# Block transposes on VectorE for denominators and clusters, a third weight buffer, and two held feed-forward pieces

## The chip, the cores and the metric

One core of a Trainium2 chip runs the whole program. The metric is the device time of one execution in microseconds, the median of several; smaller is better.

## What is computed

Two stages follow each other. The first is attention with cluster routing: 4 batches, 8 heads, 768 tokens, head size 64, 16 centroids per head. Every query and every key belongs to the cluster whose normalised centroid is nearest, and a query sees only the keys of its own cluster:

```
q_assign = argmax(q_n . c_n);  k_assign = argmax(k_n . c_n)
scores   = q k^T / sqrt(64), only where q_assign == k_assign
attn     = softmax(scores);  attn_out = attn v
```

The second stage is a feed-forward layer over the 3072 tokens, with a slope per hidden unit for negative values:

```
x = attn_out as (4*768, 512)
h = x @ w_in                                  # 512 -> 2048
g = max(h, 0) + alpha * min(h, 0)
out = g @ w_out                               # 2048 -> 512
```

The weights w_in and w_out arrive as 64-bit floats and are turned into fp32 on the chip; everything large is fp32.

## The kernel before, in words

The work is cut into 96 steps (`steps`, L313). The order is by batch, then by half of the queries (384 columns), then by pair of heads (4 pairs), then by group of two key tiles (3 groups, s = 0, 1, 2). The 12 steps of one (batch, half) are called a block here: block 0 is steps 0 to 11, block 7 steps 84 to 95, and after step 95 comes a tail. The order of all instructions is written out by hand in the loop at L498, and each engine executes its own part in that order.

What one step u puts out, in this order:

- `score(u)`: four score products into PSUM (L327, 8 TensorE instructions, since an fp32 product is two passes), then two exponentials on ScalarE (L335) into the tiles E, keys on partitions.
- `weigh(u-1)`: the products of the masked E with v, summed over the keys in PSUM tile vps (L388). At a pair's last step (s = 2) it first adds up the denominators: `sum_rows` (L368) multiplies by a matrix of ones, so that each row of the result holds the sum over all keys, repeated on 64 partitions. VectorE takes the minimum of it (L403) and the reciprocal (L405) over 128 x 384 elements.
- `mask(u)`: four VectorE instructions (L343) that compare the cluster of each query (tile aq, the query's cluster number repeated on all partitions) with the cluster of each key (a column of tile first) and multiply E by the result.
- `normalise(u-1)`: at s = 2, xT = vps * rd (L413), which writes one of the four chunks of xT, the input of the feed-forward layer.
- `add_up(u)`: from block 1 on, VectorE adds the masked E tiles into acc (L356, L361), so that `sum_rows` has one source instead of six. In block 0 `sum_rows` takes E itself.
- Then feed-forward pieces of the block before, preparation pieces of later pairs and weight conversions, interleaved one by one (L523).

Feed-forward pieces (`ffn_pieces`): per block 16 `hidden(f)` (8 instructions L434, two ScalarE instructions L441 and L442; a VectorE instruction L426 for the slope is issued with the next hidden piece) and 12 `final` (8 instructions L453 each; 8 instructions are 4 products). 28 pieces are spread over the 12 steps of the next block, 3 or 2 per step; the last block's pieces are the tail. In the pieces for the first block, four hidden pieces and three final ones alternate, because the weights are being converted at the same time; in all others, hidden pieces come first. Each `hidden` reads all four chunks of xT. Their PSUM tiles come from the pool ps_f, which has two buffers.

Preparation of a pair (only for half = 0, in the steps before it is needed): three steps ahead, transposes of q and k (`prep_features`, L241, copied by ScalarE at L245); two steps ahead, similarities with the centroids (`prep_sims`, L268, copied by ScalarE into simT, L273) and then `prep_clusters`: three TensorE transposes (L279), and VectorE finds for each token the highest similarity and the first cluster that reaches it (L285 to L294). One step ahead, and for both halves, `prep_queries` broadcasts the clusters of the queries to all partitions: three bf16 products with the identity per head (L304) and a ScalarE copy into aq (L307).

Weights (`convert`, L169): 32 pieces of 128 x 512 numbers. SP issues the transfer into a tile raw (pool raws, two buffers), VectorE takes exponent and mantissa apart (L176, L178), ScalarE converts them (L180, L182), and one conversion later VectorE completes both (L186, L189) and GpSimd multiplies them into w_in_sb or w_out_sb (L192). One conversion is issued in each of steps 1 to 11, two in each of steps 12 to 23; `convert_up_to` adds some if a feed-forward piece needs its weights sooner.

At the end a flag is computed from the largest squared norm and the smallest denominator (L531 to L541, one product at L538); TensorE has that product in its queue before the tail's pieces.

Of the kernel before, what the change touches and what calls it, by code (L numbers as in the profile page):

```python
# [21 lines left out]
def kernel(  # L22
# [43 lines left out]
    rdp = fast.enter_context(tc.tile_pool(name="rdp", bufs=2))  # L66
# [49 lines left out]
    ident_bf = const.tile([P, P], BF16, name="ident_bf")  # L116
    nc.gpsimd.tensor_copy(out=ident_bf, in_=ident)
# [15 lines left out]
    csq = const.tile([P, D], FP32, name="csq")  # L133
    cs2 = const.tile([P, 1], FP32, name="cs2")
    nc.vector.tensor_tensor(out=csq, in0=cen, in1=cen, op=ALU.mult)
    nc.vector.tensor_reduce(out=cs2, in_=csq, axis=AX.X, op=ALU.add)
# [6 lines left out]
    cn = const.tile([P, D], FP32, name="cn")  # L143
# [109 lines left out]
    NG, W = 4, 2 * NC  # L253
    GT = NB // NG
    assert NB % NG == 0 and W * NG == P and GT * P <= 512

    def slot(t, h):

        g, i = divmod(t, GT)
        return (i * NG + g) * 2 + h  # L260

    simTs = {}

    def prep_sims(n):
        hp = pairs[n][1]
        ps = misc()
        for g in range(NG):
            nc.tensor.matmul(out=ps[g * W:(g + 1) * W, 0:GT * P],  # L268
                             lhsT=cT[:, hp * W:(hp + 1) * W],
                             rhs=qkTs[n][:, g * GT * P:(g + 1) * GT * P],  # L270
                             start=True, stop=True)
        simTs[n] = asg.tile([P, GT * P], FP32, name="simT")
        nc.scalar.copy(simTs[n], ps[:, 0:GT * P])  # L273

    def prep_clusters(n):
        simT = simTs.pop(n)
        ps = misc()
        for i in range(GT):
            nc.tensor.transpose(out=ps[:, i * P:(i + 1) * P],  # L279
                                in_=simT[:, i * P:(i + 1) * P], identity=ident)  # L280
        sim = ps[:, 0:GT * P].rearrange("p (t c) -> p t c", c=NC)


        mx = asg.tile([P, 2 * NB], FP32, name="mx")
        nc.vector.tensor_reduce(out=mx, in_=sim, axis=AX.X, op=ALU.max)  # L285
        top = asg.tile([P, 2 * NB, NC], BF16, name="top")
        nc.vector.tensor_tensor(
            out=top, in0=sim, in1=mx[:, :, None].broadcast_to((P, 2 * NB, NC)),
            op=ALU.is_ge)
        nc.vector.tensor_tensor(  # L290
            out=top, in0=top, in1=rank[:, None, :].broadcast_to((P, 2 * NB, NC)),
            op=ALU.mult)
        first = fsp.tile([P, 2 * NB], BF16, name="first")
        nc.vector.tensor_reduce(out=first, in_=top, axis=AX.X, op=ALU.max)  # L294
        firsts[n] = first

    def prep_queries(n, half, h):

        if h == 0:
            aqs[n, half] = aqp.tile([P, 2, HS], BF16, name="aq")  # L300
        ps = misc()
        for i in range(HJ):
            t = slot(half * HJ + i, h)
            nc.tensor.matmul(out=ps[:, i * P:(i + 1) * P],  # L304
                             lhsT=firsts[n][:, t:t + 1].broadcast_to((P, P)),
                             rhs=ident_bf, start=True, stop=True)
        nc.scalar.copy(aqs[n, half][:, h, :], ps[:, 0:HS])  # L307
# [11 lines left out]
    def score(u):  # L319
        n, half, s = steps[u]  # L320
        qkT, first = qkTs[n], firsts[n]
# [16 lines left out]
    def mask(u):  # L338
        n, half, s = steps[u]
        for c, E in zip(range(s * GROUP, (s + 1) * GROUP), Es[u]):  # L340
            for h in range(2):
                t = slot(NJ + c, h)
                nc.vector.scalar_tensor_tensor(  # L343
                    out=E[:, h, :], in0=aqs[n, half][:, h, :],
                    scalar=firsts[n][:, t:t + 1],
                    in1=E[:, h, :], op0=ALU.is_equal, op1=ALU.mult)

    def add_up(u):
# [5 lines left out]
        if s == 0:  # L354
# [3 lines left out]
            E = E[2:]  # L358
        for e in E:
            acc = accs[n, half]  # L360
            nc.vector.tensor_tensor(out=acc, in0=acc, in1=e, op=ALU.add)  # L361

# [9 lines left out]
    def weigh(u):  # L372
# [6 lines left out]
        den = None  # L379
# [10 lines left out]
        if den is None:  # L390
            return
        if s == 0 or u >= UB:
            rds[n, half] = rdp.tile([P, HS], FP32, name="rd")
        rd = rds[n, half]
        if u < UB:
            if s == 0:
                nc.vector.tensor_copy(out=rd, in_=den[:, 0:HS])
            else:
                nc.vector.tensor_tensor(out=rd, in0=rd, in1=den[:, 0:HS], op=ALU.add)
            den = rd  # L400
        if s == SB - 1:
            i = 2 * n + half
            nc.vector.tensor_reduce(out=lowest[:, i:i + 1], in_=den[:, 0:HS], axis=AX.X,  # L403
                                    op=ALU.min)
            nc.vector.reciprocal(out=rd, in_=den[:, 0:HS])  # L405
# [89 lines left out]
    for piece in prep_at.pop(-1):  # L495
        piece()
    ffn = deque()
    for u in range(NS + 1):  # L498
# [5 lines left out]
        if u > 0:  # L504
            weigh(u - 1)
        if u < NS:
# [14 lines left out]
        take = len(ffn) - whole * (UB - 1 - u % UB) // UB if ffn else 0  # L521
# [179 lines left out]
```

## Time and profile before

| | |
|---|---|
| median of 3 runs | 1154.46 us (1152.25 to 1156.92) |
| the profiled execution | 1159.15 us |
| its span, first to last instruction | 1157.3 us |
| mean granted TensorE clock | 0.972 |
| TensorE busy | 1089.4 us, 94% |
| VectorE busy | 627.7 us, 54% |
| ScalarE busy | 390.8 us, 34% |
| GpSimd busy | 45.8 us, 4% |
| chain that ended last, by engine | PE 79%, DVE 12%, DMA 4%, ACT 3% |

PE is TensorE's products, PEld its weight loads, DVE VectorE, ACT ScalarE, POOL GpSimd, SP the engine that issues most transfers. Busy time of PE is modelled: products are pipelined, one overlaps the next, and the duration of a row of several instructions includes that overlap. The cost of a group on a full TensorE is therefore best read as the distance from its start to the start of what follows.

### The profile page before, as it was taken

What the parts mean: (1) busy time and instruction counts of PE and PEld (TensorE: products, weight loads), DVE (VectorE), ACT (ScalarE), POOL (GpSimd) and SP (SyncE); (2) the same over time, 40 slices, a digit from 0 to 9 for tenths busy, and PEclk for the clock granted to TensorE, in tenths of its full rate; (3) what the DMA queues carried; (4) which work ended last, traced back from release to release, by engine and by line L of the source; (5) the groups of instructions that cost most, each with busy time, mean ns of one, the idle gap of its engine ahead of it and who ended that gap; (6) DMA issues with size and microseconds to landing.
All of it is one profiled execution on the core that took longest, in us unless ns stands there. A gap on an engine that the chain in (4) does not pass through costs nothing.

```text
span 1157.3 us, 10680 instructions
## 1 busy us (share of the span) xinstructions
PE 1089.4 (94%) x4143; PEld 519.2 (45%) x4143; DVE 627.7 (54%) x974; ACT 390.8 (34%) x731; POOL 45.8 (4%) x58
## 2 busy tenths in 40 slices
PE   7988978879999999999999999999999999998998
PEld 4433423334554445444554445444554445443553
DVE  3898777765665356534664446545565456634210
ACT  5544433343441234223443133232443124311310
POOL 0112111120000000000000000000000000000000
PEclk8999989889999999999999999999999999999999
DMA  8122224413000100022100010021100000000000
GB/s 201 56 73 79 86 72 114 114 45 100 1 1 10 32 14 14 1 60 57 35 1 10 9 37 14 1 59 50 42 1 7 13 10 1 1 9 19 1 10 21
DMA packets 62826, 42.75 MB, mean 37 GB/s; under 512 B 51488, under 2 KB 55600, under 8 KB 62768
## 3 DMA queue, kind: packets, MB, share of 16 engines
q1 hardware_dynamic: 62592, 41.95, 13.0%
q8 instruction: 35, 0.57, 0.2%
q14 instruction: 23, 0.19, 0.1%
q10 hardware_dynamic: 176, 0.04, 0.0%
HBM read 35.69 MB, written 6.29 MB: 36 GB/s over the span
## 4 chain that ended last, share of the span: by engine, by line
PE 79%; DVE 12%; DMA 4%; ACT 3%; issue 1%; POOL 0%; DVEq 0%; ACTq 0%; POOLq 0%
PE fps L434 27%; PE fps L453 27%; PE sps L327 11%; PE vps L388 9%; DVE E L343 4%; DVE rd L405 3%; DMA raw<-in_moe_w_in_dram 2%; PE mps L368 2%; DMA raw<-in_moe_w_out_dram 2%; PE mps L241 1%; DVE mant L189 1%; DVE power L186 1%; DVE power L176 1%; PE mps L268 1%; PE mps L304 1%
## 5 line engine op out<-in xcount | busy, mean ns | idle before, releaser
L434 PE MATMUL fps<-xT,w_in_sb 128*128 128x384 f32 x1024 | 364.0, 506 | 21.4 <-DVE xT L413 17.6
L453 PE MATMUL fps<-w_out_sb,gT 128*128 128x512 f32 x768 | 353.1, 608 | 20.3 <-POOL w_out_sb L192 7.6
L343 DVE SCALAR_TENSOR_TENSOR E<-aq,first,E 128x384 f32<-128x384 bf16 x384 | 212.5, 615 | 180.1 <-ACT E L335 180.0
L434 PEld LDWEIGHTS fps<-xT,w_in_sb 128*128 128x128 f32 x1024 | 192.2, 195 | 176.1 <-issue 39.4
L453 PEld LDWEIGHTS fps<-w_out_sb,gT 128*128 128x128 f32 x768 | 142.2, 192 | 200.9 <-issue 188.4
L335 ACT ACTIVATE E<-sps 128x768 f32<-128x768 f32 x192 | 145.5, 812 | 107.1 <-PE sps L327 72.6
L441 ACT ACTIVATE gT<-fps 128x384 f32<-128x384 f32 x128 | 62.7, 490 | 303.6 <-PE fps L434 303.6
L327 PE MATMUL sps<-qkT 64*128 64x384 f32 x768 | 155.4, 524 | 1.7 <-ACT E L335 1.7
L388 PE MATMUL vps<-E,vt 128*64 128x384 f32 x768 | 144.8, 494 | 0.0
L426 DVE SCALAR_TENSOR_TENSOR gT<-neg,alpha_neg,gT 128x384 f32<-128x384 f32 x128 | 76.9, 615 | 84.8 <-ACT neg L442 84.2
L361 DVE TENSOR_TENSOR acc<-acc,E 128x768 f32<-128x768 f32 x112 | 106.9, 954 | 1.9
L327 PEld LDWEIGHTS sps<-qkT 64*128 64x128 f32 x768 | 68.1, 192 | 61.0 <-issue 29.8
L388 PEld LDWEIGHTS vps<-E,vt 128*64 128x64 f32 x768 | 52.0, 136 | 78.0 <-issue 65.1
L403 DVE TENSOR_REDUCE lowest<-mps 128x1 f32<-128x384 f32 x28 | 15.6, 556 | 124.2 <-PE mps L368 124.2
L405 DVE RECIPROCAL rd<-mps 128x384 f32<-128x384 f32 x28 | 71.3, 2547 | 0.0
L442 ACT ACTIVATE neg<-fps 128x384 f32<-128x384 f32 x128 | 62.2, 486 | 0.0
L459 ACT COPY y<-fps 128x512 f32<-128x512 f32 x24 | 14.0, 584 | 137.6 <-PE fps L453 137.6
L180 ACT ACTIVATE power<-power,low_exp 128x512 uint32<-128x512 uint32 x32 | 23.1, 723 | 96.3 <-DVE power L176 96.3
L307 ACT CAST aq<-mps 128x384 bf16<-128x384 f32 x57 | 27.5, 482 | 52.6 <-PE mps L304 52.5
L245 ACT COPY qkT<-mps 128x512 f32<-128x512 f32 x40 | 23.6, 590 | 24.1 <-PE mps L241 24.1
L176 DVE TENSOR_SCALAR power<-raw 128x512 uint32<-128x512 uint32 x32 | 13.5, 422 | 32.1 <-DMA raw<-in_moe_w_out_dram 18.1
L304 PEld LDWEIGHTS <-first 128*128 128x128 bf16 x192 | 15.5, 99 | 31.0 <-issue 22.9
(81 smaller groups left out, 460.6 us busy)
## 6 DMA issues: line engine op xcount, KB each, us to landing
raw<-in_moe_w_in_dram SPq DMA_DIRECT2D x16, 512.0 KB, 3.9
raw<-in_moe_w_out_dram SPq DMA_DIRECT2D x16, 512.0 KB, 3.5
qk<-in_q_dram SPq DMA_DIRECT2D x32, 192.0 KB, 3.5
qk<-in_k_dram SPq DMA_DIRECT2D x32, 192.0 KB, 3.9
vt<-in_v_dram SPq DMA_DIRECT2D x16, 384.0 KB, 4.3
out_dram<-y SPq DMA_DIRECT2D x24, 256.0 KB, 2.0
cen<-in_centroids_dram ACTq DMA_DIRECT2D x1, 32.0 KB, 1.9
alf<-in_moe_alpha_dram ACTq DMA_DIRECT2D x1, 8.0 KB, 2.5
```

The source lines that it names most:

```text
L307: nc.scalar.copy(aqs[n, half][:, h, :], ps[:, 0:HS])
L327: nc.tensor.matmul(out=ps[:, h, 0:HS], lhsT=qkT[r:r + D, S + c * P:S + (c + 1) * P], rhs=qkT[r:r + D, half * HS:(half + 1) * HS], start=Tr ...
L335: nc.scalar.activation(out=E, in_=ps[:, :, 0:HS], func=AF.Exp, scale=SCALE)
L343: nc.vector.scalar_tensor_tensor(out=E[:, h, :], in0=aqs[n, half][:, h, :], scalar=firsts[n][:, t:t + 1], in1=E[:, h, :], op0=ALU.is_equal ...
L361: nc.vector.tensor_tensor(out=acc, in0=acc, in1=e, op=ALU.add)
L388: nc.tensor.matmul(out=po[r:r + D, 0:HS], lhsT=vts[n][:, h, c, :], rhs=e[:, h, :], start=(c == 0), stop=(c == NJ - 1))
L405: nc.vector.reciprocal(out=rd, in_=den[:, 0:HS])
L426: nc.vector.scalar_tensor_tensor(out=gs[f], in0=neg, scalar=alpha_neg[:, f:f + 1], in1=gs[f], op0=ALU.mult, op1=ALU.add)
L434: nc.tensor.matmul(out=ps[:, 0:HS], lhsT=w_in_sb[:, c, f * P:(f + 1) * P], rhs=xT[:, c, :], start=(c == 0), stop=(c == NCH - 1))
L441: nc.scalar.activation(out=gs[f], in_=ps[:, 0:HS], func=AF.Relu)
L442: nc.scalar.activation(out=neg, in_=ps[:, 0:HS], func=AF.Relu, scale=-1.0)
L453: nc.tensor.matmul(out=ps[:, 0:DM], lhsT=gs[f][:, i * P:(i + 1) * P], rhs=w_out_sb[:, f, :], start=on and f == f0, stop=off and f == f0 + ...
```

## The change

Four things, in one edit:

- **Denominators.** From block 1 on, `add_up` ends a pair's last step with a VectorE transpose of acc in blocks of 32 x 32 (128 x 768 elements) and a sum over the 32 elements of each block row (tile part, 128 x 24). A new function `denominators`, called right after `weigh`, multiplies part by a constant matrix fold (ones where two partitions agree modulo 32), one product of 24 columns. VectorE takes reciprocal and minimum of the 24 columns and makes rd from them by two block transposes of a broadcast (64 x 384 each). `sum_rows` stays for block 0.
- **Clusters.** `prep_sims` no longer goes through ScalarE and TensorE: VectorE transposes the similarities out of PSUM by blocks and finds the clusters at once. `prep_clusters` now spreads the result over all partitions by four small bf16 products with constant matrices, a ScalarE copy (tile every), and a product and maximum on VectorE (tile key). `prep_queries` becomes one VectorE block transpose of a broadcast per head, bf16, 128 x 384. `mask` takes its scalar from key.
- **Weights.** The pool raws has three buffers instead of two. The pools aqp, asg and rdp have one buffer less each.
- **Held pieces.** KEEP = 2: the last two feed-forward pieces of a block (both of them final pieces) stay in the list when the block ends and are the first to be issued in the next one. So block 1 issues 26 of its 28 pieces, and the tail has 30.

At the start, constants fold, spread and own are made by GpSimd, and TensorE's 40 bf16 warm-up products become 10 fp32 ones.

```
-    aqp = fast.enter_context(tc.tile_pool(name="aqp", bufs=3))
-    asg = fast.enter_context(tc.tile_pool(name="asg", bufs=2))
-    raws = fast.enter_context(tc.tile_pool(name="raws", bufs=2))
+    aqp = fast.enter_context(tc.tile_pool(name="aqp", bufs=2))
+    asg = fast.enter_context(tc.tile_pool(name="asg", bufs=1))
+    raws = fast.enter_context(tc.tile_pool(name="raws", bufs=3))
-    rdp = fast.enter_context(tc.tile_pool(name="rdp", bufs=2))
+    rdp = fast.enter_context(tc.tile_pool(name="rdp", bufs=1))
...
-    for i in range(40):
-        nc.tensor.matmul(out=warm[:, 0:P], lhsT=ident_bf, rhs=ident_bf, start=True,
-                         stop=True)
+    for i in range(10):
+        nc.tensor.matmul(out=warm[:, 0:P], lhsT=ident, rhs=ident, start=True, stop=True)
...
     def prep_sims(n):
...
-        simTs[n] = asg.tile([P, GT * P], FP32, name="simT")
-        nc.scalar.copy(simTs[n], ps[:, 0:GT * P])
-
-    def prep_clusters(n):
-        simT = simTs.pop(n)
-        ps = misc()
-        for i in range(GT):
-            nc.tensor.transpose(out=ps[:, i * P:(i + 1) * P],
-                                in_=simT[:, i * P:(i + 1) * P], identity=ident)
-        sim = ps[:, 0:GT * P].rearrange("p (t c) -> p t c", c=NC)
+        simT = asg.tile([P, HS], FP32, name="simT")
+        nc.vector.transpose(out=simT, in_=ps[:, 0:HS])
+        sim = simT.rearrange("p (t c) -> p t c", c=NC)
...
+    def prep_clusters(n):
+        first = firsts.pop(n)
+        ps = misc()
+        for g in range(NG):
+            nc.tensor.matmul(out=ps[:, g * 2 * NX:(g + 1) * 2 * NX], lhsT=spread[:, g, :],
+                             rhs=first, start=True, stop=True)
+        every = fsp.tile([P, NG, GT, NG, 2], BF16, name="every")
+        nc.scalar.copy(every.rearrange("p g i r h -> p (g i r h)"),
+                       ps[:, 0:NG * 2 * NX])
+        mine = asg.tile([P, NG * GT, NG, 2], BF16, name="mine")
+        nc.vector.tensor_tensor(
+            out=mine, in0=every.rearrange("p g i r h -> p (g i) r h"),
+            in1=own[:, None, :, None].broadcast_to((P, NG * GT, NG, 2)), op=ALU.mult)
+        key = fsp.tile([P, NB, 2], BF16, name="key")
+        nc.vector.tensor_reduce(out=key, in_=mine.rearrange("p t r h -> p t h r"),
+                                axis=AX.X, op=ALU.max)
+        everys[n], keys[n] = every, key
+
     def prep_queries(n, half, h):
...
-        ps = misc()
-        for i in range(HJ):
-            t = slot(half * HJ + i, h)
-            nc.tensor.matmul(out=ps[:, i * P:(i + 1) * P],
-                             lhsT=firsts[n][:, t:t + 1].broadcast_to((P, P)),
-                             rhs=ident_bf, start=True, stop=True)
-        nc.scalar.copy(aqs[n, half][:, h, :], ps[:, 0:HS])
+        own_half = everys[n].rearrange("p g i r h -> p g (i r) h")[:, half, :, h:h + 1]
+        nc.vector.transpose(out=aqs[n, half][:, h, :],
+                            in_=own_half.broadcast_to((P, NX, Q)))
...
-                    scalar=firsts[n][:, t:t + 1],
+                    scalar=keys[n][:, NJ + c, h:h + 1],
...
+        if s == SB - 1:
+            accT = accp.tile([P, 2 * NX, Q], FP32, name="acc")
+            nc.vector.transpose(out=accT.rearrange("p x i -> p (x i)"),
+                                in_=acc.rearrange("p h q -> p (h q)"))
+            part = rdp.tile([P, 2 * NX], FP32, name="part")
+            nc.vector.tensor_reduce(out=part, in_=accT, axis=AX.X, op=ALU.add)
+            parts[n, half] = part
+
+    def denominators(u):
+        n, half, s = steps[u]
+        if s < SB - 1 or u < UB:
+            return
+        ps = misc()
+        nc.tensor.matmul(out=ps[:, 0:2 * NX], lhsT=fold, rhs=parts.pop((n, half)),
+                         start=True, stop=True)
+        inv = rdp.tile([P, 2 * NX], FP32, name="inv")
+        nc.vector.reciprocal(out=inv, in_=ps[:, 0:2 * NX])
+        i = 2 * n + half
+        nc.vector.tensor_reduce(out=lowest[:, i:i + 1], in_=ps[:, 0:2 * NX], axis=AX.X,
+                                op=ALU.min)
+        rd = rdp.tile([P, HS], FP32, name="rd")
+        for h in range(2):
+            r = slice(h * D, (h + 1) * D)
+            nc.vector.transpose(
+                out=rd[r, :],
+                in_=inv[r, h * NX:(h + 1) * NX, None].broadcast_to((D, NX, Q)))
+        rds[n, half] = rd
...
-        elif s == SB - 1:
-            den = sum_rows([accs.pop((n, half))])
...
+    KEEP = 2
...
             weigh(u - 1)
+            denominators(u - 1)
...
-            assert not ffn
...
-            whole = len(ffn)
+            whole = len(ffn) - KEEP
...
-        take = len(ffn) - whole * (UB - 1 - u % UB) // UB if ffn else 0
+        take = (max(len(ffn) - KEEP - whole * (UB - 1 - u % UB) // UB, 0) if ffn else 0)
```

## Rows read from the trace of the kernel before

**Rows 1.** Busy time by stretch: length, PE, PEld, DVE, ACT, POOL, clock, DMA, GB/s.

```profile
16.16:93.70 77.54, 67.65 (x366) 30.90 (x365) 63.97 (x114) 44.24 (x77) 10.55 (x9) 0.95 0.29 87
93.70:266.00 172.30, 141.58 (x483) 64.17 (x483) 122.92 (x205) 66.25 (x121) 33.48 (x24) 0.91 0.29 84
266.00:400.50 134.50, 132.31 (x527) 63.55 (x525) 73.13 (x109) 46.77 (x91) 0.00 (x0) 1.00 0.09 24
400.50:531.50 131.00, 128.81 (x483) 60.92 (x481) 68.99 (x100) 40.56 (x76) 0.00 (x0) 0.99 0.09 25
...
sum 1157.30, PE 1089.39 PEld 519.24 DVE 627.71 ACT 390.85 POOL 45.80; mean PE 108.94 PEld 51.92 DVE 62.77 ACT 39.08 POOL 4.58
```

**Rows 2.** Waits, 105 to 266 us: total, times, longest.

```profile
DVE power L176 <- DMA raw<-in_moe_w_out_dram: 18.1, 6, 3.7
...
DVE power L176 <- DMA raw<-in_moe_w_in_dram: 12.8, 4, 4.0
...
DVE y L461 <- PE fps L453: 11.8, 5, 5.0
```

**Rows 3.** Order of time, block 1: start, duration, engine, line, [idle before].

```profile
153.23 0.43 DVE L176 TENSOR_SCALAR power<-raw 128x512 uint32<-128x512 uint32 x1 [3.48 <-DMA raw<-in_moe_w_in_dram]
...
154.84 0.47 ACT L441 ACTIVATE gT<-fps 128x384 f32<-128x384 f32 x1
...
155.79 1.96 PE L453 MATMUL fps<-w_out_sb,gT 128*128 128x512 f32 x4 [3.20 <-issue]
```

**Rows 4.** Order of time of TensorE, block 6 (half = 0).

```profile
806.59 0.91 PE L434 MATMUL fps<-xT,w_in_sb 128*128 128x384 f32 x2 [2.19 <-DVE xT L413]
...
833.67 0.87 PE L368 MATMUL mps<-acc,ones 128*64 128x384 f32 x4
...
834.37 1.46 PE L388 MATMUL vps<-E,vt 128*64 128x384 f32 x8
```

**Rows 5.** Order of time, TensorE, end of block 4 and block 5.

```profile
663.92 3.65 PE L453 MATMUL fps<-w_out_sb,gT 128*128 128x512 f32 x8
...
667.67 1.56 PE L327 MATMUL sps<-qkT 64*128 64x384 f32 x8
...
675.64 7.77 PE L434 MATMUL fps<-xT,w_in_sb 128*128 128x384 f32 x18 [2.19 <-DVE xT L413]
...
683.34 1.56 PE L327 MATMUL sps<-qkT 64*128 64x384 f32 x8
...
691.62 1.56 PE L327 MATMUL sps<-qkT 64*128 64x384 f32 x8
...
700.30 1.56 PE L327 MATMUL sps<-qkT 64*128 64x384 f32 x8
...
711.82 1.56 PE L327 MATMUL sps<-qkT 64*128 64x384 f32 x8
```

**Rows 6.** Busy time of one stretch, columns as in rows 1.

```profile
675.60:683.40 7.80, 7.76 (x20) 4.18 (x20) 2.08 (x3) 1.74 (x4) 0.00 (x0) 0.78 0.01 2
```

**Rows 7.** Instruction groups: count, busy us, mean ns, idle before.

```profile
L397 DVE COPY rd<-mps 128x384 f32<-128x384 f32 x2 | 1.1, 552 | 3.2 <-PE mps L368 3.2
...
L361 DVE TENSOR_TENSOR acc<-acc,E 128x768 f32<-128x768 f32 x112 | 106.9, 954 | 1.9
...
L403 DVE TENSOR_REDUCE lowest<-mps 128x1 f32<-128x384 f32 x28 | 15.6, 556 | 124.2 <-PE mps L368 124.2
...
L405 DVE RECIPROCAL rd<-mps 128x384 f32<-128x384 f32 x28 | 71.3, 2547 | 0.0
...
L279 PE MATMUL mps<-ident,simT 128*128 128x128 f32 x42 | 7.3, 286 | 2.3 <-ACT simT L273 2.3
```

**Rows 8.** Order of time of VectorE: masks, block 1 and block 6.

```profile
128.39 2.88 DVE L343 SCALAR_TENSOR_TENSOR E<-aq,first,E 128x384 f32<-128x384 bf16 x4 [0.47 <-ACT E L335]
...
803.96 2.10 DVE L343 SCALAR_TENSOR_TENSOR E<-aq,first,E 128x384 f32<-128x384 bf16 x4
```

**Rows 9.** Order of time of TensorE, end of the attention steps.

```profile
1066.32 0.19 PE L538 MATMUL mps<-ones,good 128*1 128x1 f32 x2 [3.12 <-DVE good L535]
```

More of the change, by code (lines that the diff above doesn't have):

```diff
@@ L115 @@
     make_identity(nc, ident)
-    ident_bf = const.tile([P, P], BF16, name="ident_bf")
-    nc.gpsimd.tensor_copy(out=ident_bf, in_=ident)
+    Q = 32
+    fold = const.tile([P, P], FP32, name="fold")
+    spread = const.tile([P, P // Q, P], BF16, name="spread")
+    nc.gpsimd.memset(spread, 0.0)
+    for g in range(P // Q):
+        r = slice(g * Q, (g + 1) * Q)
+        nc.gpsimd.tensor_copy(
+            out=fold[r, :].rearrange("p (a i) -> p a i", i=Q),
+            in_=ident[r, None, r].broadcast_to((Q, P // Q, Q)))
+        nc.gpsimd.tensor_copy(out=spread[r, g, :], in_=fold[r, :])
+    own = const.tile([P, P // Q], BF16, name="own")
+    nc.gpsimd.memset(own, 0.0)
+    for g in range(P // Q):
+        nc.gpsimd.memset(own[g * Q:(g + 1) * Q, g:g + 1], 1.0)
     ones = const.tile([P, D], FP32, name="ones")
@@ L250, in prep_features @@
                                      accum_out=squares[:, 2 * n + w:2 * n + w + 1])
-    NG, W = 4, 2 * NC
+    NG, W = P // Q, 2 * NC
     GT = NB // NG
[L255 to L262, printed above, removed]
+    NX = GT * NG
+    assert NB % NG == 0 and W == Q and GT == HJ and NX * Q == HS
+    everys, keys = {}, {}
     def prep_sims(n):
@@ L285, in prep_clusters @@
+        mx = asg.tile([P, 2 * NX], FP32, name="mx")
         nc.vector.tensor_reduce(out=mx, in_=sim, axis=AX.X, op=ALU.max)
-        top = asg.tile([P, 2 * NB, NC], BF16, name="top")
+        top = asg.tile([P, 2 * NX, NC], BF16, name="top")
         nc.vector.tensor_tensor(
-            out=top, in0=sim, in1=mx[:, :, None].broadcast_to((P, 2 * NB, NC)),
+            out=top, in0=sim, in1=mx[:, :, None].broadcast_to((P, 2 * NX, NC)),
             op=ALU.is_ge)
         nc.vector.tensor_tensor(
-            out=top, in0=top, in1=rank[:, None, :].broadcast_to((P, 2 * NB, NC)),
+            out=top, in0=top, in1=rank[:, None, :].broadcast_to((P, 2 * NX, NC)),
@@ L292, in prep_clusters @@
             op=ALU.mult)
-        first = fsp.tile([P, 2 * NB], BF16, name="first")
+        first = asg.tile([P, 2 * NX], BF16, name="first")
         nc.vector.tensor_reduce(out=first, in_=top, axis=AX.X, op=ALU.max)
         firsts[n] = first
+    def prep_clusters(n):
[15 more added lines that the diff above has]
+        everys[n], keys[n] = every, key
@@ L320, in score @@
         n, half, s = steps[u]
-        qkT, first = qkTs[n], firsts[n]
+        qkT = qkTs[n]
         pss = []
@@ L358, in add_up @@
             E = E[2:]
+        acc = accs[n, half]
         for e in E:
-            acc = accs[n, half]
             nc.vector.tensor_tensor(out=acc, in0=acc, in1=e, op=ALU.add)
+        if s == SB - 1:
[5 more added lines that the diff above has]
+            parts[n, half] = part
+    parts = {}
+    def denominators(u):
[17 more added lines that the diff above has]
+        rds[n, half] = rd
     def sum_rows(srcs):
@@ L389, in weigh @@
                                  rhs=e[:, h, :], start=(c == 0), stop=(c == NJ - 1))
-        if den is None:
+        if u >= UB:
             return
-        if s == 0 or u >= UB:
+        if s == 0:
             rds[n, half] = rdp.tile([P, HS], FP32, name="rd")
         rd = rds[n, half]
[L395 to L400, printed above, removed]
+        if s == 0:
+            nc.vector.tensor_copy(out=rd, in_=den[:, 0:HS])
+        else:
+            nc.vector.tensor_tensor(out=rd, in0=rd, in1=den[:, 0:HS], op=ALU.add)
         if s == SB - 1:
             i = 2 * n + half
-            nc.vector.tensor_reduce(out=lowest[:, i:i + 1], in_=den[:, 0:HS], axis=AX.X,
+            nc.vector.tensor_reduce(out=lowest[:, i:i + 1], in_=rd, axis=AX.X,
                                     op=ALU.min)
-            nc.vector.reciprocal(out=rd, in_=den[:, 0:HS])
+            nc.vector.reciprocal(out=rd, in_=rd)
     def normalise(u):
```

14 lines of the change are left out of this document (5 added, 9 removed).

## The prediction

> **What bounds the kernel now.** I read the busy time by stage first. Over the whole span TensorE is busy 1089 of 1157 us, so it looks like the bound everywhere, but the stages differ [rows 1]. "Block" means the 12 steps of one (batch, half). In block 2 (266.0 to 400.5) TensorE is busy for 132.3 of 134.5 us and VectorE for 73: TensorE's queue is full, and a microsecond taken out of it is a microsecond of time. In block 1 (93.7 to 266.0), which also converts 24 weight pieces, TensorE is busy for only 141.6 of 172.3 us at a granted clock of 0.91, while VectorE has 122.9. In block 0 (16.2 to 93.7) VectorE is the fullest engine, 64.0 of 77.5 us.
>
> The waits of block 1 come next: VectorE waits 18.1 + 12.8 = 30.9 us for weight transfers at L176 [rows 2]. The order of time shows what one such wait does: VectorE idles 3.48 us, ScalarE (whose next instruction needs that result) evacuates a feed-forward tile only at 154.84, and TensorE, which lacked that PSUM buffer, stands still for 3.20 us [rows 3]. With two raw buffers the second conversion of a step can request its words only when the conversion before it has ended.
>
> Last come the block ends. TensorE reaches chunk 3 of xT 2.2 us before VectorE has written it [rows 4, 5]. In the three blocks with half = 1 more is lost: the 18 instructions behind the wait take 7.77 us [rows 5], the granted clock of that stretch is 0.78 [rows 6], so part of it ran at the lower of the two levels (1.2 against 2.4 GHz).
>
> **Part 1, TensorE, blocks 2 to 7.**
> - The row sums of acc (L368) take 834.37 - 833.67 = 0.70 us [rows 4], 24 times: 16.8 us.
> - The query broadcasts (L304): in one block two adjacent steps, otherwise alike, take 691.62 - 683.34 = 8.28 and 700.30 - 691.62 = 8.68 us, the second with the broadcasts of two heads [rows 5]. 0.40 x 24 = 9.6 us.
> - The sim transposes (L279): 42 instructions are 14 pairs, 7.3 us busy, 0.52 each [rows 7]; they overlap their neighbours a little, so 0.45 x 12 = 5.4 us.
> - The block ends. Half = 1: step 0 takes 15.67 us (667.67 to 683.34), step 3 with the same TensorE work 11.52 (700.30 to 711.82) [rows 5]: 4.15 x 3 = 12.5. Half = 0: the wait of 2.19 alone [rows 4], x 3 = 6.6. The cover: a final piece takes 3.5 us (663.92 to 667.67, less 0.2 of one head's broadcast) [rows 5], two held ones 7.0; VectorE needs, after the fold, about 0.2 + 0.2 + 2 x 0.5 for inverse, minimum and two transposes, then 2.10 of mask [rows 8] and 0.55 of xT (as long as the 0.55 of [rows 7]), 4.1 in all. All 19.1 goes; what is late next is nothing here, with some 3 us to spare. Without that cover the 19.1 stays.
>
> Together -50.9 us. Added to the same queue:
> - 24 folds, two passes with 24 columns each. The nearest row is the flag product, two passes with one column, 0.19 us [rows 9]; the far one the 0.70 that it replaces. I take 0.25, near the first, for its few columns: 6 us (4.6 to 16.8).
> - 12 spreads, four small bf16 products, which have the columns of less than one query broadcast: 0.25 each, 3 us (1 to 5).
> - Waits. The spread needs `first`, and now only one feed-forward piece stands between sims and spread on TensorE. VectorE's chain there is a slope operation behind the sims (0.6), a transpose, two reductions and two comparisons or products, about 3.2 us at the 0.55 of such rows [rows 7]. A final piece (3.5) covers it, a hidden piece (8 instructions, 2.6 us) does not. Two of the three preparations in each half = 0 block stand beside hidden pieces: 6 x 0.7 = 4.2 us (0 to 12). Behind the waiting spread stand the next scores, and behind those the exponentials and masks, so the wait is paid in full.
>
> Part 1: -50.9 + 13.2 = -37.7 us.
>
> **Part 2, VectorE.** No block transpose is in this trace. Nearest rows for 384 elements per partition: copy out of PSUM 0.55; for 768, an addition 0.95; the dear end is the reciprocal, 2.55 for 384 [rows 7]; the cheap end I put at half the copy. I take 0.5 and 0.9, the copy being nearest in kind. The Trainium skill, VectorE: DVE Perf Modes, section "The three transpose paths", gives 311 ns for 128 bf16 columns; an estimate for 384 with the slope of these rows is 0.56, and the sum would be some 3 us higher by it. No run here shows that price.
>
> Per (pair, half) the minimum and reciprocal go (0.56 + 2.55) [rows 7] and 0.9 + 0.95 + 0.4 + 1.0 come: no change. The queries add 2 x 0.47, and a pair's preparation adds 1.0 (transpose, `mine`, `key`), over the kernel 45 us. In blocks 2 to 7 some 60 us per block are free on VectorE, so this costs nothing; without that room it would show as waits of TensorE for masks. In ScalarE's queue the copies of aq and simT go, off the path.
>
> **Part 3, block 1.** A third raw buffer lets each transfer start one conversion earlier. About 4 us are to be hidden [rows 3], and between two such starts lie a conversion (2.2) and mask plus additions (over 4): the 30.9 us of waits go. SP's queue keeps its order: a word transfer that waits there for its buffer holds back the loads of the next pairs and no more, and those are needed some steps later. What takes their place: VectorE's 122.9 becomes about 128.5 (+7 of queries and preparation, -1.4 for two additions to y that move on). Its other idle time is 172.3 - 122.9 - 30.9 = 18.5 us, 11.8 of it waits for TensorE's finals [rows 2], which should shrink as TensorE stops stalling. There is also contention: four masks take 2.88 us beside a GpSimd multiply and 2.10 without one [rows 8]. The twelve multiplies that used to run while VectorE waited now run beside its work: 12 x 0.4 = 5. So block 1 is at least 133.5 and at most 152; I take 147: -25 us (-41 if TensorE alone bounds it, -5 if little is won).
> The skill's page SBUF — State Buffer, section "SBUF: two separate sides", says that of these two engines the loser of the shared port pair blocks for the other's whole instruction. The 0.78 us of these rows is a loss of that sort; whole multiplies lost each time would put block 1 some 10 us higher.
>
> **Part 4, the held pieces.** Two pieces move out of block 1, which TensorE does not bound, into the tail, which it does: +7.0 us there, -0.4 for the fold. The wait for the flag product (3.12) [rows 9] stays, since the held pieces are issued behind it.
>
> **Part 5, block 0 and the start.** The old denominators stay there. VectorE, already the fullest, gets four query sets and three preparations, 6.8 us, and TensorE issues the next scores only after `first`, a microsecond or so: +8 us (0 to +14). At the start GpSimd builds four more constants, hidden by the first loads; 10 fp32 products in place of 40 bf16 ones are as long.
>
> **Sum:** -37.7 + 6.6 - 25 + 8 = -48 us. The profiled execution took 1159.15, 4.7 above the median of 1154.46; I take the difference from the median: **1106 us**.
>
> **Rivals.**
> - *TensorE bounds block 1 entirely.* Block 3 holds the same TensorE work in 131 us [rows 1]. For it: VectorE's waits were mostly consequences. Against: VectorE alone needs 133. 1090 us, chance 0.18.
> - *The conversions stay the bound* through VectorE's queue and the shared port: block 1 wins 7 instead of 25. For it: the 2.88 against 2.10. 1124 us, chance 0.20.
> - *Block ends are not covered*, because the fold comes late and VectorE's chain starts later: 19 us stay. 1125 us, chance 0.05.
> - *Block transposes are dear*, 1.0 us for 384 elements: 37 such units in blocks 0 and 1 cost 18 more, 12 waits for `first` 6 more. 1130 us, chance 0.08.
> - *Slower.* The same place, decided at 1.5 us per 384 elements: (37 + 12) x 1.0 eats the 48. At the reciprocal's 2.55, 49 x 2.05 gives 1206 us. Against it: a transpose does not iterate as a reciprocal does; nothing here shows one. Chance 0.05.
>
> The forecast itself has 0.44. Its own range is 1097 to 1115; with the neighbours and the bounds of block 1 and block 0 the range is **1080 to 1140**. A measurement of this kernel tells about 0.5% from no change: faster 0.92, same 0.03, slower 0.05.
>
> **What would show it.** Right: no wait of L176 on transfers; block 1 near 147; steps 1 and 2 of a block shorter by about 0.4; no wait for xT from block 2 on and no 0.78 stretch there; a tail 6 to 7 us longer. Wrong: block transposes over 1 us, TensorE waiting at the spread for more than 1 us each time, block 1 above 160, block 0 above 92.

## The result and the profile after

The changed kernel takes 1117.39 us (median of four runs, 1116.98 to 1121.12); the kernel before, run beside it, 1155.4 (1152.25 to 1156.92). The ratio is 0.9682, interval 0.9652 to 0.9712: faster by 3.2%. The prediction was 1106, range 1080 to 1140.

The profiled execution took 1117.08 us. Its page starts so (busy time of each engine):

```profile
span 1115.2 us, 10299 instructions
...
PE 1054.7 (95%) x3891; PEld 500.4 (45%) x3891; DVE 693.2 (62%) x1198; ACT 362.2 (32%) x667; POOL 47.6 (4%) x71
```

TensorE and ScalarE have less to do, VectorE has 65 us more (627.7 before). Where that shows depends on the stage. Busy time by stretch (length, PE, PEld, DVE, ACT, POOL, granted clock, DMA, GB/s), against [rows 1]: block 0, block 1, blocks 2 and 3.

```profile
14.40:103.60 89.20, 67.68 (x348) 30.72 (x344) 70.91 (x133) 40.48 (x70) 10.56 (x9) 0.89 0.28 85
103.60:258.40 154.80, 131.51 (x440) 60.00 (x440) 133.74 (x227) 62.74 (x112) 32.29 (x24) 0.92 0.30 87
258.40:387.80 129.40, 128.53 (x497) 61.09 (x496) 84.20 (x145) 42.95 (x82) 0.00 (x0) 1.00 0.11 29
387.80:511.10 123.30, 123.30 (x449) 58.15 (x448) 76.00 (x127) 37.17 (x67) 0.00 (x0) 1.00 0.14 36
```

Measured between the blocks' first products, block 0 became longer by 11.6 us (77.58 to 89.21), block 1 shorter by 17.5 (172.30 to 154.75). The stretch from block 2 to where TensorE begins the last step's weigh went from 795.05 to 755.9 us, a gain of 39.1: TensorE has hardly a gap left there (it is busy for 123.30 of the 123.30 us of block 3). The start is 1.8 shorter, the tail 4.7 longer. Together that is -42 us between the two profiled spans; the profiled run of before lay 4.7 above its median, and the medians are 38 apart.

The waits of block 1 (total, times, longest) answer to [rows 2]:

```profile
DVE E L361 <- ACT E L354: 7.8, 7, 2.6
PE fps L498 <- DVE gT L471: 6.9, 3, 5.1
DVE power L189 <- POOL w_out_sb L205: 5.3, 5, 1.4
...
PE fps L479 <- DVE xT L458: 4.7, 1, 4.7
...
DVE power L189 <- POOL w_in_sb L205: 2.6, 3, 1.2
```

The 30.9 us of waits for weight transfers are gone. In their place the same instruction (L189 is the L176 of before) waits 7.9 us for GpSimd: the tiles power and mant have two buffers, so a conversion must wait until GpSimd has multiplied the words of the conversion two back, and that multiply was released only just before.

The order of time of TensorE at the end of block 4 and in block 5, against [rows 5], and at the end of the attention steps, against [rows 9]:

```profile
640.61 1.56 PE L346 MATMUL sps<-qkT 64*128 64x384 f32 x8
...
643.54 0.40 PE L398 MATMUL mps<-part,fold 128*128 128x24 f32 x2
643.78 7.11 PE L498 MATMUL fps<-w_out_sb,gT 128*128 128x512 f32 x16
650.74 2.74 PE L479 MATMUL fps<-xT,w_in_sb 128*128 128x384 f32 x8
653.41 1.56 PE L346 MATMUL sps<-qkT 64*128 64x384 f32 x8
...
1015.74 0.40 PE L398 MATMUL mps<-part,fold 128*128 128x24 f32 x2
1018.86 0.19 PE L585 MATMUL mps<-ones,good 128*1 128x1 f32 x2 [2.72 <-DVE good L582]
1018.98 8.83 PE L498 MATMUL fps<-w_out_sb,gT 128*128 128x512 f32 x16
```

The two held pieces (x16) run for 7 us between the fold and the first products that read xT (L479), which then wait for nothing. The fold moves its followers by 643.78 - 643.54 = 0.24 us, the predicted 0.25. In the tail the same two pieces stand behind the wait for the flag product and take 8.7 us up to the next product (1027.64) instead of 7.0.

What the new VectorE instructions cost (groups: count, busy us, mean ns, idle before), which no row of before could show:

```profile
L325 DVE STREAM_TRANSPOSE aq<-every 128x384 bf16<-128x384 bf16 x64 | 34.5, 561 | 0.0
L408 DVE STREAM_TRANSPOSE rd<-inv 64x384 f32<-64x384 f32 x56 | 32.1, 572 | 0.4
L384 DVE STREAM_TRANSPOSE acc<-acc 128x768 f32<-128x768 f32 x28 | 27.4, 978 | 1.0
L387 DVE TENSOR_REDUCE part<-acc 128x24 f32<-128x768 f32 x28 | 26.7, 953 | 1.0
...
L401 DVE RECIPROCAL inv<-mps 128x24 f32<-128x24 f32 x28 | 8.6, 306 | 74.1 <-PE mps L398 74.1
```

A block transpose of 384 elements per partition costs about what the copy of 384 in [rows 7] costs (0.55 us), for bf16 and fp32 alike.

### The profile page after: what moved, and what is told of

Read it like the earlier page. It is cut to its first block, busy times and chain, and to the rows that moved or that the text cites. A ratio compares the mean times of both kernels' runs of the same rounds, so it can differ in the third digit from the quotient of the medians.

```text
span 1115.2 us, 10299 instructions
## 1 busy us (share of the span) xinstructions
PE 1054.7 (95%) x3891; PEld 500.4 (45%) x3891; DVE 693.2 (62%) x1198; ACT 362.2 (32%) x667; POOL 47.6 (4%) x71
## 3 DMA queue, kind: packets, MB, share of 16 engines
q1 hardware_dynamic: 62592, 41.95, 13.5%
## 4 chain that ended last, share of the span: by engine, by line
PE 74%; DVE 19%; ACT 4%; issue 2%; POOL 1%; DVEq 0%; ACTq 0%; POOLq 0%
PE fps L498 26%; PE fps L479 25%; PE sps L346 10%; PE vps L435 9%; DVE E L361 6%; DVE acc L379 2%; PE mps L254 1%; ACT qk L262 1%; ACT E L354 1%; DVE rd L450 1%; DVE mant L202 1%; DVE power L199 1%; PE mps L398 1%; DVE power L189 1%; DVE top L290 1%
## 5 line engine op out<-in xcount | busy, mean ns | idle before, releaser
L479 PE MATMUL fps<-xT,w_in_sb 128*128 128x384 f32 x1024 | 354.5, 498 | 9.7 <-DVE y L506 5.0
L498 PE MATMUL fps<-w_out_sb,gT 128*128 128x512 f32 x768 | 348.1, 605 | 7.1 <-DVE gT L471 6.9
L361 DVE SCALAR_TENSOR_TENSOR E<-aq,key,E 128x384 f32<-128x384 bf16 x384 | 216.5, 626 | 185.8 <-ACT E L354 184.9
L479 PEld LDWEIGHTS fps<-xT,w_in_sb 128*128 128x128 f32 x1024 | 191.1, 192 | 156.5 <-issue 24.4
L435 PE MATMUL vps<-E,vt 128*64 128x384 f32 x768 | 147.3, 498 | 0.5 <-DVE xT L458 0.5
L379 DVE TENSOR_TENSOR acc<-acc,E 128x768 f32<-128x768 f32 x112 | 107.0, 955 | 1.9
L401 DVE RECIPROCAL inv<-mps 128x24 f32<-128x24 f32 x28 | 8.6, 306 | 74.1 <-PE mps L398 74.1
L325 DVE STREAM_TRANSPOSE aq<-every 128x384 bf16<-128x384 bf16 x64 | 34.5, 561 | 0.0
L408 DVE STREAM_TRANSPOSE rd<-inv 64x384 f32<-64x384 f32 x56 | 32.1, 572 | 0.4
L254 PE MATMUL mps<-ident,qk 128*128 128x128 f32 x160 | 25.1, 281 | 5.4 <-ACT qkT L258 4.5
L254 PEld LDWEIGHTS mps<-ident,qk 128*128 128x128 f32 x160 | 20.4, 145 | 20.3 <-issue 10.9
```

What stands on the lines that cost most here:

```text
L254: nc.tensor.transpose(out=ps[:, i * P:(i + 1) * P], in_=raw_qk[n, w][:, j].rearrange("p h d -> p (h d)"), identity=ident)
L325: nc.vector.transpose(out=aqs[n, half][:, h, :], in_=own_half.broadcast_to((P, NX, Q)))
L361: nc.vector.scalar_tensor_tensor(out=E[:, h, :], in0=aqs[n, half][:, h, :], scalar=keys[n][:, NJ + c, h:h + 1], in1=E[:, h, :], op0=ALU.is ...
L435: nc.tensor.matmul(out=po[r:r + D, 0:HS], lhsT=vts[n][:, h, c, :], rhs=e[:, h, :], start=(c == 0), stop=(c == NJ - 1))
L479: nc.tensor.matmul(out=ps[:, 0:HS], lhsT=w_in_sb[:, c, f * P:(f + 1) * P], rhs=xT[:, c, :], start=(c == 0), stop=(c == NCH - 1))
L498: nc.tensor.matmul(out=ps[:, 0:DM], lhsT=gs[f][:, i * P:(i + 1) * P], rhs=w_out_sb[:, f, :], start=on and f == f0, stop=off and f == f0 + ...
```

## The experiments

All kernels here compute the whole result. Ratios are to the kernel before, run beside each. It took 1155.21 us beside experiments 1, 3, 6 and 7, 1151.27 beside 2, 5, 8 and 10, and 1153.79 beside 4, 9 and 11; differences of medians across these are good to a few us, and the ratios decide.

**1. Two raw buffers again.**

```
-    raws = ... tc.tile_pool(name="raws", bufs=3)
+    raws = ... tc.tile_pool(name="raws", bufs=2)
```

> The changed kernel with two raw buffers again. Theory (the third buffer removed the transfer waits of block 1, and VectorE's own work is what is left there): VectorE waits about 30 us for weight words again, block 1 grows from 154.8 to 175-183 us, the whole by 20 to 28 us. Rival (the transfers are hidden in this order of work; block 1 got shorter through the reciprocals, the copies and the two pieces that left it): block 1 stays within 5 us of 154.8.

Measured: 1141.81 us, ratio 0.9874 (0.9838 to 0.991), 24.4 over the changed kernel. Block 1 takes 174.63 us, 19.9 more; block 0 94.42, 5.2 more; the rest is as it was. VectorE's waits in block 1:

```profile
DVE power L189 <- DMA raw<-in_moe_w_out_dram: 17.6, 6, 3.7
DVE power L189 <- DMA raw<-in_moe_w_in_dram: 13.3, 5, 3.9
```

The waits for transfers are back, 30.9 us in this stretch. The 5.2 us of block 0 are not such waits (there they are 0.6 us in all): its granted clock is 0.84. In the other runs whose block 0 is that of the changed kernel it takes 89.2 to 91.7, so up to 5 of the 24.4 us have another cause, which stays open. Without the third buffer the edit gains 1.3% instead of 3.2%.

**2. The third buffer alone**, in the kernel before (aqp and asg give the room, as in the change).

> The kernel before with three raw buffers and nothing else (aqp and asg give up one buffer each to make room). Theory (the transfer waits of block 1 are on the path by themselves): L176 waits for transfers no more, block 1 shrinks from 172 to 145-152 us, the whole by 20 to 27 us. Rival (the prefetch pays only together with the work that the change takes off ScalarE and VectorE): under 10 us.

Measured: 1130.62, ratio 0.9824 (0.9808 to 0.984), 20.7 below the kernel before. Block 1 falls to 151.6 us, with no wait for transfers, and has 9.7 us of waits for GpSimd: these come with the third buffer, not with the new cluster path.

**3. Nothing held over a block's end.**

```
-    KEEP = 2
+    KEEP = 0
```

> The changed kernel without held pieces (KEEP = 0). Theory (the held pieces cover the way from the fold to xT at the block ends): TensorE waits about 2.3 us for xT at six block ends, with a stretch at the lower clock behind some of them, 14 to 20 us in all; the tail gets 7 us shorter and block 1 0 to 5 us longer; the whole 8 to 16 us slower. Rival (the shorter way through the denominators alone closes the gap, the held pieces only move work into the tail): 2 to 7 us faster.

Measured: 1137.83, ratio 0.9861 (0.9835 to 0.9887), 20.4 over the changed kernel, more than expected. TensorE's waits from block 2 on:

```profile
PEld fps L479 <- DVE xT L458: 17.3, 6, 2.9
PE fps L479 <- DVE xT L458: 13.6, 6, 2.3
```

Six block ends, one wait of up to 2.3 us each. The short denominator chain alone doesn't close the gap. Blocks with half = 0 are 3.1 us longer and those with half = 1 2.5 to 4.2, block 1 2.9; the tail gives 6.9 back.

**4. Pieces held, in the kernel before**, with nothing else changed (KEEP = 2 and the same two lines that use it).

> The kernel before with KEEP = 2 alone. Theory: the held pieces are worth the block ends wherever the denominators come from, for the two pieces (7.0 us) cover sum_rows' chain too (minimum 0.56, reciprocal 2.55, two masks, xT: some 6 us). Blocks 2 to 6 fall by 2 to 4 us each, block 1 loses up to 7 of its pieces but is bound by the transfers (within 3 us of 172), the tail is 5 to 7 longer: the whole 8 to 16 us under the kernel before. Rival: without the short chain of the new denominators the xT waits of 2.2 us stay, and the tail's 7 us make it as slow as before or slower.

Measured: 1136.64, ratio 0.9864 (0.9836 to 0.9892), 17.2 below the kernel before, just over the expected 8 to 16. Blocks take 132.0 and 126.8 us (134.5 and 131), and no wait for xT is left from block 2 on, so 7 us of cover are enough for sum_rows and the long reciprocal too. Block 1 falls by 6.4, which I had not expected; which part of it is the two pieces fewer wasn't separated.

**5. Old denominators** in the changed kernel: add_up, weigh and normalise as before, no fold.

> The changed kernel with the denominators of before (sum_rows, minimum and reciprocal of 128 x 384); clusters, three raw buffers and held pieces stay. Theory (the fold gives 0.42 us of TensorE per pair and half, and the held pieces cover the longer way through reciprocals too): blocks 2 to 7 longer by 24 x 0.42 = 10 us, no wait for xT at the block ends, block 1 within 3 us; the whole 8 to 12 us slower. Rival (the shorter way to xT is what the denominators are worth): waits for xT come back, 15 us slower or more.

Measured: 1126.62, ratio 0.979 (0.9774 to 0.9806): 9.2 slower than the changed kernel by medians, 12.5 by the ratios; its span is 7.4 us longer. No wait for xT came back. Blocks 2 to 6 are 1.7 longer each, which is 4 times the 0.42 between fold and row sums. Block 1 is 3.4 shorter: there the new denominators cost VectorE more than the old (133.7 us busy against 130.7).

**6. The old cluster path** in the changed kernel: TensorE's sim transposes and query broadcasts with ScalarE's copies, as before; the rest stays.

```
+        nc.scalar.copy(simTs[n], ps[:, 0:GT * P])
...
+            nc.tensor.transpose(out=ps[:, i * P:(i + 1) * P],
+                                in_=simT[:, i * P:(i + 1) * P], identity=ident)
...
-        nc.vector.transpose(out=aqs[n, half][:, h, :],
-                            in_=own_half.broadcast_to((P, NX, Q)))
+        nc.scalar.copy(aqs[n, half][:, h, :], ps[:, 0:HS])
```

> The changed kernel with the clusters of the kernel before (TensorE transposes, query broadcasts by TensorE with ScalarE copies); denominators, three raw buffers and held pieces stay. Theory (the cluster part pays in blocks 2 to 7 what it costs in blocks 0 and 1): block 0 back to 77-80 us, block 1 4 to 8 us shorter, blocks 2 to 7 about 11 us longer in all; the whole between 6 us faster and 2 us slower. Rival (the cluster part is a net gain of the size of the TensorE work that it removes): 8 us slower or more.

Measured: 1107.14, ratio 0.9584 (0.9552 to 0.9617), 10.2 **below** the changed kernel, more than the 6 expected at most. The cluster part of the edit is a loss. TensorE's order of time in block 0 shows where, first in the changed kernel, then with the old path:

```profile
44.37 0.84 PE L278 MATMUL fps<-qkT,cT 128*32 128x384 f32 x4 [0.40 <-ACT qkT L258]
45.68 0.84 PE L278 MATMUL fps<-qkT,cT 128*32 128x384 f32 x4 [0.47 <-ACT qkT L258]
52.11 0.28 PE L306 MATMUL fps<-first,spread 128*128 128x24 bf16 x4 [5.59 <-DVE first L297]
52.32 2.93 PE L346 MATMUL sps<-qkT 64*128 64x384 f32 x8
```

```profile
43.29 0.84 PE L279 MATMUL fps<-qkT,cT 128*32 128x384 f32 x4 [0.47 <-ACT qkT L253]
45.90 0.68 PE L290 MATMUL mps<-ident,simT 128*128 128x128 f32 x3 [1.76 <-ACT simT L284]
46.50 2.93 PE L338 MATMUL sps<-qkT 64*128 64x384 f32 x8
```

Between sims (L278) and the next step's first products the old path waits for one ScalarE copy; the chain to first then runs on VectorE beside that step. The new path holds TensorE until first itself is there, 5.59 us. The three steps of block 0 with a preparation grew from 6.15, 10.13 and 10.14 us in the kernel before to 8.67, 14.83 and 14.85: 11.9 us, all that block 0 lost. The old path's block 0 is 76.43, its block 1 149.41 (VectorE 128.15 busy); blocks 2 to 6 are 0.9 or 1.8 us longer than the changed kernel's.

**7. The spread one step later.**

```
-            at(2, lambda n=n: prep_clusters(n))
+            at(1, lambda n=n: prep_clusters(n))
```

> The changed kernel with prep_clusters one step later, so that TensorE's spread no longer stands right behind the sims. Theory (block 0 lost 11.6 us, 6.8 of it VectorE's added work and the rest TensorE's wait for first, which delays the next scores and through them the masks): block 0 shrinks from 89.2 to 82-86 us, step 1 of the half = 0 blocks by 0.4, the whole by 4 to 8 us. Rival (VectorE's work alone sets block 0, TensorE's wait at the spread is slack): block 0 stays within 1.5 us, the whole within 2 us.

Measured: 1108.81, ratio 0.9604 (0.9581 to 0.9628), 8.6 below the changed kernel. The same spread of block 0, then the busy time of that block:

```profile
51.13 0.26 PE L306 MATMUL mps<-first,spread 128*128 128x24 bf16 x4 [0.51 <-DVE first L297]
```

```profile
14.30:97.68 83.38, 65.29 (x348) 29.73 (x345) 72.15 (x134) 40.08 (x70) 10.58 (x9) 0.98 0.31 93
```

5.59 became 0.51; block 0 is 5.8 shorter at a granted clock of 0.98 instead of 0.89, and the blocks with half = 0 from block 4 on are 1.1 shorter. Block 0 is still 7 us longer than with the old path; VectorE's load there, 72.15 us against 64.16, accounts for a difference of that size.

**8. Late spread, and the held pieces ahead of the flag product.**

```
+    for _ in range(KEEP):
+        ffn.popleft()()
     flag = misc()
```

> prep_clusters one step later, and the two held pieces issued before the flag is computed, so that they cover TensorE's wait for it. Theory (the 2.7 us of wait at the flag product and the slower pieces behind it, 16 instructions in 8.7 instead of 6.9 us, are on the path): 4 to 5 us below the kernel with late clusters alone (1108.8), about 1104.5. Rival (the clock drops anyway and the wait reappears elsewhere): within 1.5 us of it.

Measured: 1105.8, ratio 0.9609 (0.9593 to 0.9625). From the start of the last step's weigh to the end it is 96.5 us (1004.37 to 1100.87) against 100.9 in the changed kernel:

```profile
1006.05 7.11 PE L498 MATMUL fps<-w_out_sb,gT 128*128 128x512 f32 x16
1013.10 0.19 PE L587 MATMUL mps<-ones,good 128*1 128x1 f32 x2
```

No wait, and the pieces take 7.1. The profile shows the 4.4 us; the ratio to the kernel before is that of experiment 7, so at the level of the runs this step is inconclusive.

**9. The two conversions of a step moved apart** in block 1, to take the wait for GpSimd away without a buffer. (A third buffer for power and mant was not tried.)

```
             mask(u)
+        if UB <= u < 2 * UB:
+            convert_next()
...
-        converting = 1 if 0 < u < UB else 2 if UB <= u < 2 * UB else 0
+        converting = 1 if 0 < u < 2 * UB else 0
```

> The changed kernel with the two conversions of a block-1 step moved apart: one right behind the masks, one where both were (no buffer added, same work). Theory: what kept block 1 at 154.8 us instead of the 147 predicted is a new queue, VectorE waiting for GpSimd's multiplies (7.9 us in all) because a conversion starts on buffers whose multiply was released only one instruction earlier. With 2 us of additions or masks in between, those waits should fall under 2 us and block 1 should shorten by 3 to 7 us, to 148 to 152; the whole by as much. Rival: the waits only fill time in which VectorE would have waited for ScalarE or TensorE anyway; then the waits go and block 1 stays within 1.5 us of 154.8. Second rival: the conversion ahead of the sums and xT delays the next users of acc and y, and block 1 is longer by 2 or more.

Measured: 1122.33, ratio 0.9734 (0.9708 to 0.976), 4.9 over the changed kernel. The waits for GpSimd are gone, every one, and block 1 is 157.40, 2.7 longer. Block 0, which the edit leaves alone, is 2.5 longer in this profile too (91.67), so the 2.7 by itself is no more than two runs can differ by; what shows the collision is the rows, and experiment 11. VectorE and GpSimd around one conversion, first in the changed kernel, then moved apart:

```profile
133.72 1.27 POOL L205 TENSOR_TENSOR w_out_sb<-mant,power 128x512 f32<-128x512 f32 x1 [10.50 <-DVE mant L202]
135.03 0.43 DVE L189 TENSOR_SCALAR power<-raw 128x512 uint32<-128x512 uint32 x1 [1.38 <-POOL w_out_sb L205]
...
140.27 1.94 DVE L379 TENSOR_TENSOR acc<-acc,E 128x768 f32<-128x768 f32 x2
```

```profile
133.70 2.90 DVE L379 TENSOR_TENSOR acc<-acc,E 128x768 f32<-128x768 f32 x2
133.87 1.91 POOL L205 TENSOR_TENSOR w_out_sb<-mant,power 128x512 f32<-128x512 f32 x1 [8.95 <-DVE mant L202]
```

Two additions that take 1.94 us alone take 2.90 beside a multiply, and the multiply 1.91 instead of 1.27. Over the block the 16 additions of L379 went from a mean of 954 to 1370 ns and the four of L374 from 949 to 1776, 10.0 us together; the masks got 3.4 back. VectorE's busy time in block 1 rose from 133.7 to 140.2. The second rival was right in the sign and had the wrong mechanism: not later buffers, but a collision. VectorE pays for the multiply by waiting for it, or by running an addition beside it.

**10. The best of the parts:** old cluster path (TensorE transposes and broadcasts) for the first four pairs, which blocks 0 and 1 work on; VectorE's path with the late spread for the others; held pieces ahead of the flag.

```
+        if n < NCH:
+            simT = simTs.pop(n)
...
-            at(2, lambda n=n: prep_clusters(n))
+            at(2 if n < NCH else 1, lambda n=n: prep_clusters(n))
```

> A mixture: clusters by TensorE as before for the first batch (pairs 0 to 3, blocks 0 and 1), by VectorE and one step later for the others, held pieces before the flag. Theory (each form is kept where its engine has room: blocks 0 and 1 as in the kernel with the old clusters, 225.8 us together, the others as with late clusters): 1092 to 1098 us. Rival (blocks 0 and 1 gain little because the third buffer and the GpSimd waits set them): 1102 us or more.

Measured: **1094.55**, ratio 0.9507 (0.949 to 0.9523), 23 below the changed kernel by medians and about 20 by the ratios (0.0175 of 1154). It is 11 below experiment 8, which differs from it in the first batch's clusters and was run beside the same kernel; 10.1 of that are in blocks 0 and 1. Blocks 0, 1 and 3:

```profile
15.66:91.58 75.92, 65.16 (x366) 29.58 (x366) 64.03 (x115) 44.12 (x77) 10.83 (x9) 0.98 0.32 99
91.58:241.68 150.10, 128.51 (x459) 59.50 (x457) 129.56 (x218) 65.29 (x120) 33.47 (x24) 0.95 0.31 90
...
371.04:494.45 123.41, 123.41 (x450) 57.99 (x449) 75.89 (x127) 37.28 (x67) 0.00 (x0) 1.00 0.14 36
```

Each stage takes the cluster path that is shorter there.

**11. The same kernel with the conversions apart.**

> The same move in the kernel that has TensorE's old cluster path for the first batch, late clusters for the others and the held pieces ahead of the flag product (1094.6 us). Theory: its block 1 (150.1 us) falls by 3 to 6, the whole to 1088 to 1092. Rival: no change within 2 us.

Measured: 1099.01, ratio 0.9528 (0.9502 to 0.9554): 4.5 slower by medians, 2.4 by the ratios, whose intervals overlap; block 1 is 155.2 instead of 150.1. Neither the theory nor the rival came, but the collision of experiment 9, in a second kernel (VectorE busy for 135.9 us in block 1 instead of 129.6).

## Why the prediction was right, and where its terms were off

The forecast of 1106 missed by 11 us. The whole range held the time, the forecast's own (1097 to 1115) just did not: 1117 lies between the forecast and its neighbour of 1124, in which the conversions stay the bound. Block 1 decides between the two, and it won 17.5 us, where the forecast had 25 and that rival 7. By spans the sum was -48 and came out at -42: the errors are +7.5 in block 1 and +3.6 in block 0 against -1.4 in blocks 2 to 7, -1.9 in the tail and -1.8 at the start, so they cancel in part, which is luck. Most of the rest of the 11 us is that the spans compare with the profiled run of before, which lay 4.7 above its median.

- **Part 1, TensorE in blocks 2 to 7: -37.7 predicted, -39.1 measured.** The parts agree too. A step with a pair's last sums is 0.42 shorter (0.45 predicted), one with query broadcasts 0.39 (0.40). These are steps 3 and 2 of a block, not the steps 1 and 2 that the prediction gave as its sign: step 1 is unchanged with half = 1, and 0.5 longer with half = 0. Each block end is covered; with the two pieces taken away the wait for xT returned (experiment 3). The waits at the spread, put at 0.7 us for two of three preparations, are 0.55, 0.09 and 0.22 in steps 1, 4 and 7 of block 4.
- **Part 2, the block transposes.** 0.56 to 0.58 us per 384 elements against 0.5, and 0.98 against 0.9. The Trainium skill, VectorE: DVE Perf Modes, section "The three transpose paths", gives 311 ns for 128 columns of bf16; an estimate for 384 from it, with the slope of [rows 7] (0.40 us for 384 more), is 0.58 and not the 0.56 that the prediction worked out. The trace agrees with that estimate rather than with my 0.5. The dear rivals fell: no transpose of 384 elements came near 1.0. VectorE's added work over the kernel is 65.5 us (693.2 less 627.7), where the prediction had 45; 11 of it are the denominators, put at no change (98.0 us against the 71.3 + 15.6 of [rows 7]). In blocks 2 to 7 this cost nothing, as forecast.
- **Part 3, block 1: -25 predicted, -17.5 measured.** This is the term that failed in size. VectorE's busy time came out at the worked-out value (133.7 against 133.5), in part by luck, since the denominators' 3.0 us there were put at nothing; and the 30.9 us went. The step that was off is the idle time left, 147 - 133.5 = 13.5 us; it is 154.8 - 133.7 = 21.1. In it stand 7.9 us of waits for GpSimd: the prediction had named contention on GpSimd's multiplies, but not the two buffers of power and mant, the next queue of the same conversion. That these waits are the whole difference is not shown: with them gone (experiment 9) the idle time is 17.2, and the busy time 6.5 longer. In the kernels with less VectorE work there the idle time is the same: 149.4 - 128.2 = 21.3 with the old path, 151.3 - 130.7 = 20.6 with the old denominators, 150.1 - 129.6 = 20.5 in experiment 10. So in these kernels a microsecond of VectorE work in block 1 was a microsecond of time, also that of the new denominators (3.4 us). What the 13 us of idle time besides GpSimd are made of is only partly settled: 7.8 are waits for ScalarE's exponentials.
- **Contention.** I took 12 x 0.4 = 5 us. The 52 masks of block 1 have a mean of 695 ns, against 626 over the kernel: 3.6 us.
- **Part 4, the tail: +6.6 predicted, +4.7 measured.** The flag wait stayed, as said (2.72 against 3.12). The two pieces take 8.7 there, not 7.0; against that, the hidden pieces, which stood right behind the flag wait before, at a granted clock of 0.67 in their first 8.6 us, now run at full clock and take 41.3 us instead of 44.2.
- **Part 5, block 0: +8 predicted, +11.6 measured.** VectorE's extra is right (70.9 busy, from 64.0). That it was the fullest engine of block 0 is a misreading of [rows 1]: TensorE is busy for 67.65 us there, VectorE for 63.97, and neither fills the 77.54. "TensorE issues the next scores only after first, a microsecond or so" is the step that failed: the three waits are 3.4 to 5.6 us (14.6 in all), because in block 0 no feed-forward piece stands between sims and spread. I had named that for blocks 2 to 7 and left it unpriced where nothing covers it. The start, put at 0, gave 1.8 us (16.16 to 14.40); in the kernels of experiments 2 and 4, which start as the kernel before does, it is 15.15 and 14.89, so much of that is variation between runs.

The prediction never summed its terms by part. Had it done so, clusters would have stood at -9.6 - 5.4 + 3 + 4.2 in blocks 2 to 7, +8 in block 0 and +7 in block 1: a loss of some 7 us inside a large gain. Experiment 6 measures 10.2.

What each part is worth, by medians:

| part | alone in the kernel before | taken out of the changed kernel |
|---|---|---|
| third raw buffer | -20.7 | +24.4 |
| held pieces | -17.2 | +20.4 |
| denominators | not tried | +9.2 (spans: +7.4, ratios: +12.5) |
| clusters | not tried | -10.2 |

The right column sums to 43.8, against 38 for the whole: the parts may overlap a little, though the 6 us are hardly more than these differences are good to.

## What to carry to other kernels

Sum a change by its parts as well as by stages: a gain of 3% hid a part that cost 1%. Moving work to an engine pays only in the stages where that engine has room, so choose the path per stage, and where two engines form a chain, put the consumer a whole step behind the producer before pricing its wait at little (the spread's 5.59 us became 0.51). Behind each wait that a buffer removes, look for the next tile in the same chain that has as few buffers.

## What the runs showed of the hardware that was not expected

- A GpSimd multiply and a VectorE addition, both with two inputs in SBUF, did not share: they took turns. In experiment 9 the multiply starts 0.17 us after the first addition and ends at 135.78; the first addition's 0.95 us (to 134.65) plus the multiply's own 1.27 give 135.92. The second addition, which starts in between, takes 1.90 us and ends at 136.60, 0.82 after the multiply. The Trainium skill, SBUF — State Buffer, section "SBUF: two separate sides", states this as a lock held for a whole instruction, and these rows agree. The 2.88 against 2.10 of [rows 8] had shown only part of a multiply lost, for there the multiply had begun before the mask (at 128.01 and 128.39). Block transposes, which read one tile from SBUF, lost nothing beside a multiply: in the same run these two take 0.57 us each, the mean of all their kind. No run here moves the multiplies to such places, which is where they would cost VectorE nothing by these rows.

```profile
152.28 1.27 POOL L205 TENSOR_TENSOR w_out_sb<-mant,power 128x512 f32<-128x512 f32 x1 [5.23 <-DVE mant L202]
...
152.92 1.16 DVE L408 STREAM_TRANSPOSE rd<-inv 64x384 f32<-64x384 f32 x2
```

- After TensorE's waits of 3 to 6 us in block 0 the granted clock of the block is 0.89; with the waits gone (experiment 7) it is 0.98, and the same products take 65.3 us instead of 67.7. In the tail the 16 products of the held pieces, at full clock 7.1 us, take 8.8 right behind a wait of 2.72; the granted clock of that stretch is 0.80, so some of them ran at the lower of the two levels (1.2 against 2.4 GHz).
